# Squared score tiles kept in DRAM, turned, for the later query chunk of a two-batch attention and MLP kernel

## The chip, the cores and the metric

One core of one Trainium2 chip runs the whole program. The metric is the device time of one execution, in microseconds (us). It is given as the median of three runs; the profile is of one further execution.

## The reference

Shapes: two batches of 3136 rows, model width 256, query and key width 64, hidden width 1024. Everything is float32.

```
scores = (z @ z.T) / S                   # z: [2, 3136, 64], S = 3136; symmetric in query and key
attn   = maximum(scores, 0) ** 2         # so attn is symmetric too
x      = u * (attn @ v)                  # u, v: [2, 3136, 256]
h      = maximum(x @ w_in, 0)            # first MLP, 256 -> 1024
conv   = 3-tap convolution of h along the rows, one filter per hidden unit
x      = (h * sigmoid(conv)) @ w_out     # 1024 -> 256
xn     = (x - mean) / sqrt(var + 1e-6) * g_ln
out    = x + maximum(xn @ w1, 0) @ w2    # second MLP
```

## The kernel before

Each float32 operand of a matmul is kept as two float32r parts, a high part (`ah`, `vh`, ...) and the rest (`al`, `vl`, ...), and a product is the sum of two or three matmuls of such parts.

**Attention.** The 6272 queries of both batches are cut into 14 chunks of 448 (`WIDTHS`). A chunk goes over the 25 key tiles of its batch, 128 keys each; the last has 64 keys, whose high and low parts share one tile. For key tile j, `scores` issues two matmuls (L600, L601) into a PSUM tile `s` of 128 keys by 448 queries, ScalarE takes the positive part into the SBUF tile `a` (`relu`, L609), and ScalarE (L618) or in some tiles of the first four chunks VectorE (L614) squares it. ScalarE or VectorE then casts the high part `ah` (L382 and L386, lines of the helper `copy_r`) and VectorE subtracts for the low part `al` (L627). `av` adds attn times v into the PSUM tile `av`, for two halves of the model width with three matmuls each (L659, L661, L662). One key tile is thus eight matmuls of 448 columns, two of them for scores. At the chunk's end `gate_u` multiplies by u (L695).

**MLPs.** The rows are also cut into 17 blocks, 15 of 384 and two of 256 (`SIZES`). A block waits for the chunk that completes it. `mlps` goes over eight slices k of the hidden width: six matmuls up (L749 to L751), ScalarE and VectorE for the convolution, sigmoid and gate in a tile `t` (L790, L799, L807, L814, L819), the split into `gh` and `gl` (L829), and three matmuls down for each 128 rows (L765 to L767). Then come the normalisation (on PE the transposes L908) and the second MLP of the same form.

**Weights and loads.** All DMAs are issued from SyncE's queue (SP). `w_in`, `w_out`, `w1` and `w2` come as words that VectorE decodes in the first 200 us (L492 to L517); v and z are split in the same way (L474, L414). Each chunk loads its u and swaps two halves of z (`lh`, L565 and L566).

**Order.** A list scheduler, `Program`, sets the order. Every operation names its engine or engines with a planned duration, what it reads and writes, a due time, and the buffers it takes; buffers have a fixed number of places for each tag, and a buffer made with `True` as second argument is taken in the order of the program. The scheduler plays the whole kernel and emits each engine's instructions in the order it found. On the chip every queue, SP's too, runs in that order and waits at whatever is not there yet.

Of the kernel before, what the change touches and what calls it, by code (L numbers as in the profile page):

```python
# [15 lines left out]
P = 128  # L16
# [3 lines left out]
NJ = S // P + 1  # L20
ZW = NJ * P
EPS = 1e-6
WIDTHS = [448] * 7
SIZES = [3] * 15 + [2, 2]
WARM = 16
LAG0 = 70.0
# [8 lines left out]
GH = ("DVE", "ACT")  # L35
U_PLACES = 2
AH = ("ACT", "DVE")
CAPS = {"s": 3, "m": 3}
FUSED = 4, 2, 1
FLOAT = ("ACT", "POOL")  # L40
WH = ("ACT", "POOL")
VH = ("ACT", "POOL")
# [14 lines left out]
    "dve_copy": lambda n: 0.09 + 0.00048 * n,  # L57
    "dve_1": lambda n: 0.09 + 0.00048 * n,
    "dve_2": lambda n: 0.07 + 0.00108 * n,
    "dve_3": lambda n: 0.12 + 0.00108 * n,  # L60
    "pool_1": lambda n: 0.13 + 0.0009 * n,
    "pool_2": lambda n: 0.16 + 0.0026 * n,
# [200 lines left out]
def plan():  # L263

    chunks, blocks, after, q0, s = [], [], [], 0, 0
    for n in WIDTHS * NB:
        chunks.append((q0, q0 + n))  # L270
        q0 += n
    assert q0 == NT
    for n in SIZES:
        e = s + n * P
        blocks.append((s, e))
        after.append(next(c for c, (_, q1) in enumerate(chunks) if q1 > e or q1 == NT))
        s = e
    assert s == NT and set(after) == set(range(len(chunks)))
    return chunks, blocks, after
# [3 lines left out]
def attn_moe_kernel(ctx: ExitStack, tc: tile.TileContext, zt, ut, v, w_in, conv_w, w_out, g_ln, w1, w2, out):  # L283
# [10 lines left out]

    const = ctx.enter_context(tc.tile_pool(name="const", bufs=1))
    pool = ctx.enter_context(tc.tile_pool(name="work", bufs=1))
    psum = ctx.enter_context(tc.tile_pool(name="psum", bufs=1, space=PSUM))

    ident = const.tile([P, P], F32, name="ident")
# [14 lines left out]
    def maker(tag, places, where, shape, dtype):  # L314
# [5 lines left out]
    tags = {  # L320
        tag: maker(tag, places, where, shape, dtype)
        for tag, places, where, shape, dtype in (
            ("zst", 2, pool, [P, 512], F32),
            ("st", 3, pool, [P, 1024], F32),
            ("wc", 1, pool, [P, 512], U32),
            ("wn", 1, pool, [P, 512], U32),
            ("cst", 1, pool, [P, 3 * NF, 2], U32),
            ("chi", 1, pool, [P, 3 * NF], F32),
            ("clo", 1, pool, [P, 3 * NF], F32),
            ("a", 4, pool, [P, CW], F32),  # L330
            ("ah", A_PLACES, pool, [P, CW], F32R),
            ("al", A_PLACES, pool, [P, CW], F32R),
            ("lh", 2, pool, [P, CW], F32R),
# [1 line left out]
            ("xh", 1, pool, [P, 2 * XW], F32R),  # L335
            ("xl", 1, pool, [P, 2 * XW], F32R),
            ("h", 3, pool, [P, XW], F32),
            ("t", 3, pool, [P, BW], F32),
            ("gh", 3, pool, [P, BW], F32R),
            ("gl", 3, pool, [P, BW], F32R),  # L340
            ("ysb", 1, pool, [P, NTT * D], F32),
            ("xn", 3, pool, [P, D], F32),
            ("xth", 1, pool, [P, 2 * BW], F32R),
# [17 lines left out]
    def buf(tag, fixed=False, kind=None):  # L361
        if fixed:
            orders[tag] = orders.get(tag, 0) + 1
        return Buf(tag, orders[tag] if fixed else None, kind)
# [9 lines left out]
    def price(kind, n):  # L374
        return PRICE[kind](n)

    def f(ap):
        return ap.bitcast(F32)
# [11 lines left out]
        return [(e, us[e]) for e in (first, *others)]  # L390

    def dma(fn, kb, **kw):
        return op([("SP", max(0.08, kb / 190.0))], lambda e: fn(), late=2.0 + kb / 400.0, **kw)


    zp = [(o, min(o + 512, ZW)) for o in range(0, ZW, 512)]
# [189 lines left out]

    at_b = {}

    def scores(c, j, due):
        q0, q1 = chunks[c]  # L590
        n, o = q1 - q0, q0 % S
        ps, ab, lh = buf("w", kind="s"), buf("a"), lh_b[c]

        def a():
            return at(ab, "a")[:, :n]

        def mm(e):
            p = at(ps, "s")[:, :n]
            zj = hl[:, j * P : (j + 1) * P]
            nc.tensor.matmul(p, zj, hl[:, o : o + n], start=True, stop=False)  # L600
            nc.tensor.matmul(p, zj, at(lh)[:, :n], start=False, stop=True)  # L601

        lh_keys = [(lh, 0)] if c == 0 else [(lh, 0), (lh, 1)]
        op(
            [("PE", 2 * price("mm", n))], mm, reads=sorted({*hl_keys(j * P, P), *hl_keys(o, n)}) + lh_keys,
            writes=[(ps, 0)], takes=[ab], due=due, name=f"s{c}.{j}",
        )
        op(
            [("ACT", price("act_ps", n))], lambda e: nc.scalar.activation(a(), at(ps)[:, :n], AF.Relu),  # L609
            reads=[(ps, 0)], writes=[(ab, 0)], name="relu",  # L610
        )
        if c < FUSED[0] and j % FUSED[1] < FUSED[2]:
            op(
                [("DVE", price("dve_ps", n))], lambda e: nc.vector.tensor_tensor(a(), a(), at(ps)[:, :n], ALU.mult),  # L614
                reads=[(ps, 0)], writes=[(ab, 0)], name="square",
            )
        else:
            op([("ACT", price("act", n))], lambda e: nc.scalar.activation(a(), a(), AF.Square), writes=[(ab, 0)], name="square")  # L618
        ah, al = buf("ah"), buf("al") if j < NJ - 1 else None
        op(  # L620
            ways_copy(n, *AH), lambda e: copy_r(e, at(ah, "ah")[:, :n], a()),
            reads=[(ab, 0)], writes=[(ah, 0)], name="ah", port=True,
        )
        if al is not None:
            op(
                [("DVE", price("dve_2", n))],
                lambda e: nc.vector.tensor_tensor(at(al, "al")[:, :n], a(), f(at(ah)[:, :n]), ALU.subtract),  # L627
                reads=[(ab, 0), (ah, 0)], writes=[(al, 0)], name="al", port=True,
            )
        else:  # L630
            op(
                [("DVE", price("dve_2", n))],
                lambda e: nc.vector.tensor_tensor(
                    at(ah)[64:, :n], at(ab)[64:, :n], f(at(ah)[64:, :n]), ALU.subtract
                ),
                reads=[(ab, 0)], writes=[(ah, 0)], name="al", port=True,
            )
        at_b[c, j] = ah, al

    begun = set()  # L640

# [84 lines left out]
    def mlps(c, when):  # L726
# [201 lines left out]
        acc2 = shared("y") if tail else buf("y", True)  # L928
        for k in range(NF):
            ps = buf("w", kind="m")  # L930
            gh, gl = (buf("ah"), buf("al")) if beside else (buf("gh", True), buf("gl", True))
            for ways, fn, reads, due, d in up(ps, "w1", k, th, tl, n, when2(TURN + 0.02 + UP2 * k / NF)):
                op(ways, fn, reads=reads, adds=[(ps, 0)], takes=[gh, gl], due=due + 0.5 * d, name=f"h2{c}.{k}")
            op(
# [31 lines left out]
            pr.writers[k] = []  # L966

    note(("ident",))
    step = [(8 * price("mm", q1 - q0)) for q0, q1 in chunks]
    begin = [NJ * sum(step[:c]) for c in range(NC + 1)]  # L970
    lh_b[0] = buf("lh", True)
    load_z(0, 0, with_lh=lh_b[0])
    load_v(0, 0, 2)
# [6 lines left out]
        for i in range(4):  # L980
            load_w(nm, i)
    last0 = max(c for c in range(NC) if chunks[c][1] <= S)
    pace = 0.0
    for c in range(NC):
        if c == last0 + 1:
            for i in range(len(zp)):
                load_z(1, i)
            for a in range(0, NJ, 4):
                load_v(1, a, min(a + 4, NJ))
        if c:  # L990
            swap_lh(c)
        load_u(c)
        av_b[c] = buf("av", True)
        for j in range(NJ):
            t = 2 * (begin[c] + j * step[c])
            scores(c, j, t - 3.0)
            for d in range(2):
                av(c, j, d, t + d * 0.5)
        gate_u(c)
        for i in (i for i in range(NK) if after[i] == c):  # L1000
            make_x(i)
            length = (blocks[i][1] - blocks[i][0]) / NT * begin[NC]
            pace = max(pace, begin[c + 1])
            if c >= NC - 2:
                length = LENGTH[i - NK]
            lag = max(LAG1, LAG0 * (1 - c / LAG2))
            mlps(i, lambda x, pace=pace, lag=lag, length=length: 2 * (pace + lag + x * length))
            pace += length


    order = pr.order()
# [61 lines left out]
```

## Time and profile before

| what | value |
|---|---|
| median of three runs | 1152.42 us (1152.34 to 1155.17) |
| the profiled execution, its own time | 1152.26 us |
| its span, first to last instruction | 1150.3 us |
| PE (TensorE matmul) busy | 1136.2 us, 99% |
| VectorE (DVE) busy | 843.9 us, 73% |
| ScalarE (ACT) busy | 817.6 us, 71% |
| GpSimd (POOL) busy | 24.6 us, 2% |
| mean granted TensorE clock | 0.999 of full speed, the 2.4 GHz level |

Busy time is the time in which an engine has an instruction in work. Matmuls overlap in the engine, so the duration of one (0.36 us) is longer than the step from one start to the next (0.20 us); the steps are what add up. The span leaves out what lies before the first and after the last instruction, here 2.0 us.

### The profile page before, as it was taken

The page shows a single profiled execution, that of the slowest core. Times are in us where ns is not written, and L with a number is a line of the kernel's source. Part 1 is how long each engine was busy: PE and PEld are TensorE (multiplying, and loading weights), DVE is VectorE, ACT ScalarE, POOL GpSimd, SP SyncE. Part 2 cuts the span into 40 slices and gives each one's busy share as a digit, 9 for nine tenths or more (in the row PEclk, how much of TensorE's full clock was granted, in tenths as well). Part 3 has the DMA queues.
Part 4 walks back from the last instruction along what each step waited for, and adds up shares of the span by engine and source line. Part 5 has one row for each costly group of instructions (what it writes and reads, how often), then busy time and mean ns, then how long its engine had stood idle before and what let it go on. Part 6 is the DMA issues. An engine that isn't in the chain of part 4 may idle for free.

```text
span 1150.3 us, 18104 instructions
## 1 busy us (share of the span) xinstructions
PE 1136.2 (99%) x6870; PEld 1086.6 (94%) x6870; DVE 843.9 (73%) x1795; ACT 817.6 (71%) x1667; POOL 24.6 (2%) x39
## 2 busy tenths in 40 slices
PE   8999999999999999999999999999999999999998
PEld 7899999999999999999999999999999899999998
DVE  8999989948758596875848677775848576686694
ACT  7898878747767586776857667676858476785772
POOL 1000000000000000000000000000000000000000
PEclk9999999999999999999999999999999999999999
DMA  6412112100000021000000000000000000000000
GB/s 196 135 53 64 53 46 74 56 2 14 25 15 17 21 73 44 23 1 15 25 1 24 16 15 25 15 17 15 25 14 5 21 14 1 15 1 15 1 2 33
DMA packets 24823, 35.23 MB, mean 31 GB/s; under 512 B 1952, under 2 KB 20128, under 8 KB 24736
## 3 DMA queue, kind: packets, MB, share of 16 engines
q1 hardware_dynamic: 24736, 34.08, 9.8%
q8 instruction: 54, 0.88, 0.3%
q14 instruction: 33, 0.27, 0.1%
HBM read 24.67 MB, written 6.42 MB: 27 GB/s over the span
## 4 chain that ended last, share of the span: by engine, by line
PE 94%; DVE 2%; ACT 2%; issue 1%; DMA 0%; POOL 0%; DVEq 0%; POOLq 0%
PE av L659 12%; PE av L662 12%; PE av L661 11%; PE y L767 8%; PE y L765 8%; PE y L766 8%; PE s L600 5%; PE s L601 5%; PE h2ps L749 4%; PE h2ps L750 4%; PE h2ps L751 4%; PE hps L749 4%; PE hps L750 4%; PE hps L751 4%; PE tps L908 1%
## 5 line engine op out<-in xcount | busy, mean ns | idle before, releaser
L627 DVE TENSOR_TENSOR al<-a,ah 128x448 fp32r<-128x448 f32 x336 | 206.4, 622 | 90.6 <-ACT ah L382 88.2
L609 ACT ACTIVATE a<-s 128x448 f32<-128x448 f32 x350 | 185.0, 542 | 111.7 <-PE s L601 111.3
L659 PE MATMUL av<-ah,vh 128*128 128x448 f32 x700 | 258.2, 369 | 3.6 <-ACT ah L382 1.6
L662 PE MATMUL av<-ah,vl 128*128 128x448 f32 x700 | 253.8, 363 | 0.0
L661 PE MATMUL av<-al,vh 128*128 128x448 f32 x672 | 245.4, 365 | 2.7 <-DVE al L627 2.7
L618 ACT ACTIVATE a<-a 128x448 f32<-128x448 f32 x298 | 170.5, 580 | 4.0
L382 ACT CAST ah<-a 128x448 fp32r<-128x448 f32 x273 | 152.6, 568 | 6.7 <-DVE a L614 2.5
L659 PEld LDWEIGHTS av<-ah,vh 128*128 128x128 f32 x700 | 131.6, 188 | 14.3 <-ACT ah L382 3.2
L936 ACT ACTIVATE g2h<-h2ps 128x384 fp32r<-128x384 f32 (+1 forms) x136 | 65.1, 479 | 110.5 <-PE h2ps L751 106.3
L662 PEld LDWEIGHTS av<-ah,vl 128*128 128x128 f32 x700 | 131.6, 188 | 9.2
L941 DVE SCALAR_TENSOR_TENSOR g2l<-h2ps,g2h 128x384 fp32r<-128x384 f32 (+1 forms) x136 | 73.1, 540 | 89.2 <-ACT g2h L936 88.3
L661 PEld LDWEIGHTS av<-al,vh 128*128 128x128 f32 x672 | 126.5, 188 | 12.0 <-DVE al L627 5.9
L600 PE MATMUL s<-hl 128*128 128x448 f32 x350 | 128.3, 367 | 0.3 <-DVE hl L414 0.3
L601 PE MATMUL s<-lh,hl 128*128 128x448 f32 x350 | 128.0, 366 | 0.0
L765 PE MATMUL y<-w2h,g2h 128*128 128x256 f32 x392 | 110.5, 282 | 0.0
L767 PE MATMUL y<-w2h,g2l 128*128 128x256 f32 x392 | 110.2, 281 | 0.2 <-DVE g2l L941 0.2
L765 PE MATMUL y<-woh,gh 128*128 128x256 f32 x392 | 110.4, 282 | 0.0
L766 PE MATMUL y<-wol,gh 128*128 128x256 f32 x392 | 110.3, 281 | 0.0
L766 PE MATMUL y<-w2l,g2h 128*128 128x256 f32 x392 | 110.3, 281 | 0.0
L767 PE MATMUL y<-woh,gl 128*128 128x256 f32 x392 | 110.0, 281 | 0.0
L799 DVE SCALAR_TENSOR_TENSOR t<-h,cw,t 128x384 f32<-128x384 f32 (+1 forms) x136 | 81.7, 603 | 17.1 <-ACT t L790 16.1
L749 PE MATMUL hps<-xh,wih 128*128 128x386 f32 (+1 forms) x272 | 90.7, 333 | 0.7 <-DVE a L614 0.6
(113 smaller groups left out, 2283.7 us busy)
## 6 DMA issues: line engine op xcount, KB each, us to landing
u<-in_ut_dram SPq DMA_DIRECT2D x14, 448.0 KB, 3.6
out_dram<-ysb SPq DMA_DIRECT2D x15, 384.0 KB, 2.5
vst<-in_v_dram SPq DMA_DIRECT2D x11, 512.0 KB, 3.9
wst<-in_w_dram SPq DMA_DIRECT2D x8, 512.0 KB, 3.7
zst<-in_zt_dram SPq DMA_DIRECT2D x12, 256.0 KB, 2.9
lh<-hl SPq DMA_DIRECT2D x26, 112.0 KB, 2.8
wst<-in_w_in_dram SPq DMA_DIRECT2D x4, 512.0 KB, 3.8
wst<-in_w_out_dram SPq DMA_DIRECT2D x4, 512.0 KB, 3.6
```

What stands on the lines that cost most here:

```text
L600: nc.tensor.matmul(p, zj, hl[:, o : o + n], start=True, stop=False)
L601: nc.tensor.matmul(p, zj, at(lh)[:, :n], start=False, stop=True)
L609: [("ACT", price("act_ps", n))], lambda e: nc.scalar.activation(a(), at(ps)[:, :n], AF.Relu),
L618: op([("ACT", price("act", n))], lambda e: nc.scalar.activation(a(), a(), AF.Square), writes=[(ab, 0)], name="square")
L627: lambda e: nc.vector.tensor_tensor(at(al, "al")[:, :n], a(), f(at(ah)[:, :n]), ALU.subtract),
L659: nc.tensor.matmul(p, vhj, at(ah)[:, :n], start=first(b, d), stop=False, **kw)
L661: nc.tensor.matmul(p, vhj, at(al)[:, :n], start=False, stop=False, **kw)
L662: nc.tensor.matmul(p, vlj, at(ah)[:, :n], start=False, stop=False, **kw)
L749: nc.tensor.matmul(p, a, h_, start=d == 0, stop=False)
L765: nc.tensor.matmul(p, a, wh, start=first(acc, (i0 + i) // 2), stop=False, **kw)
L766: nc.tensor.matmul(p, a, wl, start=False, stop=False, **kw)
L767: nc.tensor.matmul(p, b, wh, start=False, stop=k == NF - 1, **kw)
```

## The change

The squared scores are symmetric: the tile of keys K by queries Q is the transpose of the tile of keys Q by queries K. Before, both are computed. The change makes chunks of whole key tiles: `TILES` gives 4, 4, 3, 4, 3, 3 and 4 tiles for the seven chunks of a batch, so 512, 512, 384, 512, 384, 384 and 448 queries (the last chunk ends with the half tile).

In chunk i, a key tile that lies in a later chunk is computed as before. In addition VectorE turns its `a` in blocks of 32 by 32 into a new tile `bl` (two places), and four DMAs on SP's queue (two for the half tile) write it to a DRAM tensor `turned`, each 32 keys as pieces of 32 elements (`spill`). A key tile that lies in an earlier chunk is not computed: one DMA reads 128 rows of `turned` into `a` (`land`, at most four at a time, `CAPS["ld"]`), and the two score matmuls, `relu` and the square are left out (`mirrored`). The cast, the subtraction and the six `av` matmuls stay. `turns` mixes the read tiles evenly with the computed ones. There are 146 spills (560 DMAs) and 154 landings in the kernel.

Besides, `a` has 6 places for 4 and its buffers, with `ah` and `al`, are taken in order; `st` has 2 for 3, `zst` 1 for 2, `t`, `gh` and `gl` 2 for 3 each. `FUSED` puts the square on VectorE in every fourth tile of the first two chunks, where it was every second of the first four. The scheduler's price of a DMA changes, and the blocks' operations are made after each chunk with the last three blocks at the end.

```diff
...
 NJ = S // P + 1
 ZW = NJ * P
 EPS = 1e-6
-WIDTHS = [448] * 7
+TILES = [4, 4, 3, 4, 3, 3, 4]
+SQ = 32
+MIRROR = 0
 SIZES = [3] * 15 + [2, 2]
 WARM = 16
 LAG0 = 70.0
...
 GH = ("DVE", "ACT")
 U_PLACES = 2
 AH = ("ACT", "DVE")
-CAPS = {"s": 3, "m": 3}
-FUSED = 4, 2, 1
+CAPS = {"s": 3, "m": 3, "ld": 4}
+FUSED = 2, 4, 1
 FLOAT = ("ACT", "POOL")
 WH = ("ACT", "POOL")
 VH = ("ACT", "POOL")
...
 
 
     chunks, blocks, after, q0, s = [], [], [], 0, 0
-    for n in WIDTHS * NB:
-        chunks.append((q0, q0 + n))
-        q0 += n
+    for b in range(NB):
+        for i in range(len(TILES)):
+            q1 = min(b * S + sum(TILES[: i + 1]) * P, (b + 1) * S)
+            chunks.append((q0, q1))
+            q0 = q1
     assert q0 == NT
     for n in SIZES:
         e = s + n * P
...
     tags = {
         tag: maker(tag, places, where, shape, dtype)
         for tag, places, where, shape, dtype in (
-            ("zst", 2, pool, [P, 512], F32),
-            ("st", 3, pool, [P, 1024], F32),
+            ("zst", 1, pool, [P, 512], F32),
+            ("st", 2, pool, [P, 1024], F32),
+            ("bl", 2, pool, [P, CW], F32),
...
-            ("a", 4, pool, [P, CW], F32),
+            ("a", 6, pool, [P, CW], F32),
...
-            ("t", 3, pool, [P, BW], F32),
-            ("gh", 3, pool, [P, BW], F32R),
-            ("gl", 3, pool, [P, BW], F32R),
+            ("t", 2, pool, [P, BW], F32),
+            ("gh", 2, pool, [P, BW], F32R),
+            ("gl", 2, pool, [P, BW], F32R),
...
 
     at_b = {}
 
+    per = len(TILES)
+    start_of = [sum(TILES[:i]) for i in range(per + 1)]
+    chunk_of = [i for i, n in enumerate(TILES) for _ in range(n)]
+
+    def mirrored(c, j):
+
+        b, i = divmod(c, per)
+        return chunk_of[j] < i and (b > 0 or chunk_of[j] >= MIRROR)
+
+    def spilled(c, j):
+        b, i = divmod(c, per)
+        return chunk_of[j] > i and mirrored(b * per + chunk_of[j], start_of[i])
+
+    turned = {}
+    for c in range(NC):
+        i = c % per
+        rows = S - start_of[i + 1] * P
+        if rows > 0:
+            turned[c] = dram.tile([P * TILES[i], rows], F32, tag=f"turned{c}", name="turned")
+
+    def spill(c, j, ab):
+        w = chunks[c][1] - chunks[c][0]
+        b = buf("bl")
+        op(
+            [("DVE", price("dve_turn", w))], lambda e: nc.vector.transpose(at(b, "bl")[:, :w], at(ab)[:, :w]),
+            reads=[(ab, 0)], writes=[(b, 0)], name="bl", port=True,
+        )
+        k0 = (j - start_of[c % per + 1]) * P
+
+        def write(e):
+            blocks_ = at(b)[:, :w].rearrange("p (b k) -> p b k", k=SQ)
+            for o in range(0, min(P, S - j * P), SQ):
+                dst = turned[c][:, k0 + o : k0 + o + SQ].rearrange("(b q) k -> q b k", q=SQ)
+                nc.sync.dma_start(out=dst, in_=blocks_[o : o + SQ])
+
+        op([("SP", 1.85)], write, reads=[(b, 0)], writes=[("turned", c, j)], late=2.2, due=1e4, name="spill")
+
+    def land(c, j):
+        q0, q1 = chunks[c]
+        n, i = q1 - q0, chunk_of[j]
+        src = c - c % per + i
+        k0 = (start_of[c % per] - start_of[i + 1]) * P
+        r0 = (j - start_of[i]) * P
+        b = buf("a", True, kind="ld")
+        op(
+            [("SP", 0.7)],
+            lambda e: nc.sync.dma_start(out=at(b, "land")[:, :n], in_=turned[src][r0 : r0 + P, k0 : k0 + n]),
+            late=2.4, writes=[(b, 0)], name="land",
+            reads=[("turned", src, jj) for jj in range(start_of[c % per], start_of[c % per + 1])],
+        )
+        return b
+
     def scores(c, j, due):
         q0, q1 = chunks[c]
-        n, o = q1 - q0, q0 % S
-        ps, ab, lh = buf("w", kind="s"), buf("a"), lh_b[c]
+        n = q1 - q0
+        from_dram = mirrored(c, j)
+        ab = land(c, j) if from_dram else buf("a", True)
 
         def a():
             return at(ab, "a")[:, :n]
+
+        if not from_dram:
+            products(c, j, ab, a, due)
+        ah, al = buf("ah", True), buf("al", True) if j < NJ - 1 else None
+        op(
+            ways_copy(n, *AH), lambda e: copy_r(e, at(ah, "ah")[:, :n], a()),
+            reads=[(ab, 0)], writes=[(ah, 0)], name="ah", port=True,
+        )
+        if spilled(c, j):
+            spill(c, j, ab)
...
+        at_b[c, j] = ah, al
+
+    def products(c, j, ab, a, due):
+        q0, q1 = chunks[c]
+        n, o = q1 - q0, q0 % S
+        ps, lh = buf("w", kind="s"), lh_b[c]
 
         def mm(e):
             p = at(ps, "s")[:, :n]
...
             )
         else:
             op([("ACT", price("act", n))], lambda e: nc.scalar.activation(a(), a(), AF.Square), writes=[(ab, 0)], name="square")
...
-        at_b[c, j] = ah, al
 
     begun = set()
 
...
             pr.writers[k] = []
 
     note(("ident",))
-    step = [(8 * price("mm", q1 - q0)) for q0, q1 in chunks]
-    begin = [NJ * sum(step[:c]) for c in range(NC + 1)]
+
+    def work(c, j):
+        n = chunks[c][1] - chunks[c][0]
+        return (6 if mirrored(c, j) else 8) * price("mm", n)
+
+    def turns(c):
+
+        old = [j for j in range(NJ) if mirrored(c, j)]
+        new = [j for j in range(NJ) if not mirrored(c, j)]
+        both = [((i + 1) / (len(x) + 0.5), x is old, j) for x in (old, new) for i, j in enumerate(x)]
+        return [j for *_, j in sorted(both)]
+
+    lengths = [sum(work(c, j) for j in range(NJ)) for c in range(NC)]
+    begin = [sum(lengths[:c]) for c in range(NC + 1)]
     lh_b[0] = buf("lh", True)
     load_z(0, 0, with_lh=lh_b[0])
     load_v(0, 0, 2)
...
             swap_lh(c)
         load_u(c)
         av_b[c] = buf("av", True)
-        for j in range(NJ):
-            t = 2 * (begin[c] + j * step[c])
+        t0 = begin[c]
+        for j in turns(c):
+            t = 2 * t0
+            t0 += work(c, j)
             scores(c, j, t - 3.0)
             for d in range(2):
                 av(c, j, d, t + d * 0.5)
         gate_u(c)
         for i in (i for i in range(NK) if after[i] == c):
-            make_x(i)
             length = (blocks[i][1] - blocks[i][0]) / NT * begin[NC]
             pace = max(pace, begin[c + 1])
             if c >= NC - 2:
                 length = LENGTH[i - NK]
             lag = max(LAG1, LAG0 * (1 - c / LAG2))
-            mlps(i, lambda x, pace=pace, lag=lag, length=length: 2 * (pace + lag + x * length))
+            when[i] = lambda x, pace=pace, lag=lag, length=length: 2 * (pace + lag + x * length)
             pace += length
+        for i in (i for i in when if i < NK - 3 and after[i] == c):
+            make_x(i)
+            mlps(i, when[i])
+    for i in range(NK - 3, NK):
+        make_x(i)
+        mlps(i, when[i])
 
 
     order = pr.order()
```

## Rows read from the trace of the kernel before

**Rows 1.** Page, part 1: busy time, share of the span, instructions.
```profile
PE 1136.2 (99%) x6870; PEld 1086.6 (94%) x6870; DVE 843.9 (73%) x1795; ACT 817.6 (71%) x1667; POOL 24.6 (2%) x39
```

**Rows 2.** Windows: length, busy (count) of PE, PEld, DVE, ACT, POOL; clock, DMA share, GB/s.
```profile
0.00:14.00 14.00, 11.22 (x50) 9.83 (x51) 9.93 (x18) 9.36 (x17) 1.58 (x9) 1.00 0.64 204
14.00:60.00 46.00, 43.12 (x205) 37.71 (x205) 44.50 (x93) 37.24 (x77) 1.80 (x3) 1.00 0.49 147
60.00:230.00 170.00, 168.97 (x944) 159.40 (x943) 160.99 (x338) 143.08 (x296) 4.44 (x6) 1.00 0.19 58
230.00:1100.00 870.00, 866.65 (x5300) 833.93 (x5299) 596.56 (x1262) 604.98 (x1221) 15.29 (x19) 1.00 0.06 17
1100.00:1150.30 50.30, 46.19 (x378) 45.77 (x377) 31.97 (x90) 22.88 (x59) 1.50 (x2) 0.98 0.06 20
```

**Rows 3.** Waits of PE: longest in total first; us, times, longest.
```profile
PE av L661 <- DVE al L627: 2.7, 7, 0.5
PE av L659 <- ACT ah L382: 1.6, 3, 0.7
```

**Rows 4.** Timeline near 61 us: start, us, engine, line, operation.
```profile
60.48 0.36 PE L600 MATMUL s<-hl 128*128 128x448 f32 x1
...
61.49 0.36 PE L601 MATMUL s<-lh,hl 128*128 128x448 f32 x1
...
61.69 0.34 PE L749 MATMUL hps<-xh,wih 128*128 128x386 f32 x1
...
63.63 0.34 PE L751 MATMUL hps<-xh,wil 128*128 128x386 f32 x1
```

**Rows 5.** Groups by line and shape: busy us, mean ns; idle before, releaser.
```profile
L609 ACT ACTIVATE a<-s 128x448 f32<-128x448 f32 x350 | 185.0, 542 | 111.7 <-PE s L601 111.3
L618 ACT ACTIVATE a<-a 128x448 f32<-128x448 f32 x298 | 170.5, 580 | 4.0
L627 DVE TENSOR_TENSOR al<-a,ah 128x448 fp32r<-128x448 f32 x336 | 206.4, 622 | 90.6 <-ACT ah L382 88.2
L614 DVE TENSOR_TENSOR a<-a,s 128x448 f32<-128x448 f32 x52 | 31.8, 617 | 3.2 <-ACT a L609 3.1
L386 DVE CAST ah<-a 128x448 fp32r<-128x448 f32 x77 | 30.5, 397 | 26.5 <-ACT a L618 25.3
```

**Rows 6.** The same view, 256-row blocks: first and last of seven groups.
```profile
L790 ACT ACTIVATE t<-h,cw 128x256 f32<-128x256 f32 x16 | 8.1, 508 | 0.3
...
L829 DVE TENSOR_TENSOR gl<-t,gh 128x256 fp32r<-128x256 f32 x16 | 6.3, 421 | 0.2
```

**Rows 7.** DMA in the window 449.5:450.4: packets; queue, MB, share of 16 engines.
```profile
DMA packets 144, 0.07 MB, mean 73 GB/s; under 512 B 16, under 2 KB 144, under 8 KB 144
q1 hardware_dynamic: 144, 0.07, 24.9%
```

**Rows 8.** The same in the window 264.4:266.0, one store of `ysb`.
```profile
DMA packets 400, 0.39 MB, mean 246 GB/s; under 512 B 16, under 2 KB 400, under 8 KB 400
q1 hardware_dynamic: 400, 0.39, 73.8%
```

**Rows 9.** Page, parts 3 and 6: the queue over the span; issues, KB, us to landing.
```profile
q1 hardware_dynamic: 24736, 34.08, 9.8%
...
out_dram<-ysb SPq DMA_DIRECT2D x15, 384.0 KB, 2.5
...
zst<-in_zt_dram SPq DMA_DIRECT2D x12, 256.0 KB, 2.9
```

**Rows 10.** Timeline of SP's queue: start, us, line of the issue.
```profile
468.46 0.49 SPq L565 DMA_DIRECT2D lh<-hl  x1
469.00 0.59 SPq L566 DMA_DIRECT2D lh<-hl  x1
```

**Rows 11.** Waits of SP's queue: us, times, longest.
```profile
SPq L955 <- DVE ysb L949: 533.0, 15, 70.9
```

**Rows 12.** Timeline of DVE: the gates that end the first two chunks.
```profile
52.68 1.16 DVE L695 SCALAR_TENSOR_TENSOR u<-av,u 128x448 f32<-128x448 f32 x2
...
103.30 1.16 DVE L695 SCALAR_TENSOR_TENSOR u<-av,u 128x448 f32<-128x448 f32 x2 [0.17 <-PE av L662]
```

## What the change does to the time: the prediction

> **What bounds the kernel now.** I read the page's busy shares first, then the windows by stage, then what PE waits for, then a stretch of the timeline, and last the transfers. PE is busy for 99% of the span, at the full clock, VectorE for 73% and ScalarE for 71% [rows 1]. By stage: PE is idle for 2.8 us of the first 14 and 2.9 us of the next 46, for about 1 us up to 230, for 3 us of the 870 after that, and for 4 us at the end [rows 2]. The longest waits of PE on one line come to 2.7 us [rows 3]. A busy PE could still be a waiting one, so the step from one start to the next decides. Six score matmuls of 448 columns start 1.01 us apart from first to last, five steps of 0.202 us; twelve of 386 columns need 1.94 us, eleven steps of 0.176 us [rows 4]. That is (0.202 - 0.176)/62 = 0.41 ns for each column more, and nothing stands between the matmuls. So PE's own work sets the end, and a matmul left out is worth its whole step, unless something new makes PE wait.
>
> VectorE is nearly as full in one place: up to 230 us it is busy 9.9 + 44.5 + 161.0 = 215.4 us, 94%, and ScalarE 189.7 us, 82%; from 230 to 1100 us they stand at 69% and 70% [rows 2]. In the first stage v, z and the weights are split beside the attention. The new work must pass there.
>
> **What it removes.** In chunk i the tiles of the earlier chunks are read: 0, 4, 8, 11, 15, 18, 21 tiles of 512, 512, 384, 512, 384, 384, 448 columns, 77 tiles and 32,832 columns for a batch, 154 and 65,664 in all, 426 columns on average. Each saves two matmuls of 0.202 - 22 x 0.00041 = 0.193 us: 308 x 0.193 = 59.4 us of PE. The other matmuls keep their number and their total of columns, since there are still seven chunks of 25 tiles. ScalarE loses relu and square of those columns, (542 + 580)/448 = 2.50 ns each [rows 5], 164 us, and takes over 39 squares (52 before, 13 after) of 0.58 us, 23 us. It is not the bound, so this counts as nothing.
>
> **What VectorE gains.** 146 turns: the spilled tiles of a batch are 21, 17, 10 of 512 and 14, 7, 4 of 384, together 68,352 columns in the kernel. The trace has no such instruction. The cheapest row that reads and writes a tile of this size is the cast, 397/448 = 0.89 ns a column, a subtraction costs 622/448 = 1.39 [rows 5]. I take 1.39, since nothing says that a turn goes at the cast's faster rate: 95 us (61 at the cast's). Nothing bounds it above; for the range I double it, 190. The squares give back 32 - 9 = 23 us. So VectorE comes to 844 + 95 - 23 = 916 us of some 1100, 83%: enough on the average.
>
> The Trainium skill (VectorE: DVE Perf Modes, The three transpose paths) gives 311 ns for a 128x128 bf16 turn on VectorE in blocks of 32. By its 2.43 ns a column the turns would come to an estimated 166 us, 31 us more of them in the first stage, and the sum below to an estimated 1137 at most; no row here shows one.
>
> In the first stage, up to 230 us, lie the first four chunks. Their turns: 48 tiles of 512 and 14 of 384, 29,952 columns, 42 us; the squares give back 23 us. VectorE's 215 us become 234, less up to 8 us of casts that ScalarE could take, where PE would need 230 less the 10 us saved in these chunks (23 tiles read, 10,752 columns, two matmuls at 0.45 ns). VectorE is over by 6 to 14 us. Part can be put off, because MLP work may run later, where VectorE has room. PE has nothing to fill chunk 0 with, as no MLP runs until its gate is done (at 52.7 us before [rows 12], with the first MLP matmul at 61.7 [rows 4]).
>
> **Behind the turns.** A place of `bl` is held for the turn (0.7 us), four issues at 0.54 us each from start to start [rows 10] and a landing of about 2.5 us like a store's [rows 9]: 5.4 us, so two places pass a tile every 2.7 us. Chunk 0 has 21 spills, 57 us, against 198 matmuls of 0.228 us = 45 us and about 14 us of start. When `bl` is full, the next turn waits on VectorE; behind it stand the subtractions of the next tiles, and PE waits for those. Six places of `a` take up part of it. For both effects, which overlap, I take 10 us, between 0 and 25.
>
> **The transfers.** A spilled tile of 512 columns is 2,048 pieces of 128 bytes, 128 for each of the 16 engines; all spills are 262,656 pieces. The trace shows larger packets: 144, mostly of 512 bytes, took 0.249 x 0.9 us x 16/144 = 25 ns each [rows 7], 400 of 1 KB, a store, 0.738 x 1.6 x 16/400 = 47 ns [rows 8]. The line through both gives 8 ns at 128 bytes. Bounds are 8 and 47; I take 15, between the line and the nearest row. Then a tile costs 1.9 us of all engines, the spills 246 us. With the landings (33.6 MB, as much as the 34.1 MB that now take 9.8% of the engines [rows 9]) the share rises from 10% to about 42%. Chunk 0 needs 20.5 x 1.9 = 39 us of its 59: hidden. At 25 ns it needs 66 us, 7 us too many, which the 10 above hold.
>
> SP issues 560 + 154 DMAs more at 0.54 us, 386 us of 1100. Its queue waits long today, up to 71 us for an `ysb` [rows 11], with little behind it. Now spills and landings stand behind such waits. A landing has four places, and 256 KB land in 2.9 us [rows 9], less than the 3.3 us that a tile and its share of MLP take (1150 us, 14 chunks of 25 tiles). I take 0, and up to 10 us in the range.
>
> **Fewer places.** With two places of `t`, `gh`, `gl` for three, a slice k of a 256-row block takes 3.13 us from the first tap to `gl` (seven groups, the first 508, the last 421 ns [rows 6]), so one slice in 1.57 us, and PE needs 12 matmuls of about 0.12 us, 1.44. Beside attention this is covered; in the last 50 us, 16 slices lose 2 us and the waits between engines something: 3 us, 0 to 8. `zst` and `st` with a place less delay loads in the first stage only; that is in the 10.
>
> **Sum.** Profiled execution 1152.3 (span 1150.3 and 2.0 around it; the median, 1152.4, is the same). 1152.3 - 59.4 + 10 + 3 = 1105.9, so 1106 us, 4.0% faster. With every loss at its lower end 1093; with 25, 10 and 8 us lost, 1136.
>
> **Rivals.**
> 1. *VectorE is the bound for a quarter of the kernel.* If a turn costs twice 1.39 ns a column, the first stage gets 42 us more on an engine that is already over. At chunks 7 and 8 (38 tiles, then 54 us of turns in some 180 us) 30% come on top of 69%. Of the 42 us I take 30 as lost and 5 at chunks 7 and 8: 1106 + 35 = 1141. For it: 94% before 230 us. Against it: the scheduler may put MLP work off.
> 2. *Slower: the small pieces choke the DMA engines.* The place is `bl` in the chunks that spill most. At 47 ns a piece, chunk 0 needs 123 us of the engines against 59, chunk 1 99 against about 56 (it took 51 with 448 columns [rows 12]), chunk 2 61 against 50, chunk 7 123 against 94 (82 x 512/448), chunk 8 99 against 92: 64 + 43 + 11 + 29 + 7 = 154 us lost in place of the 10, time 1250. It decides from about 36 ns on, where chunks 0 and 1 lose 35 + 20 us, which with the 3 of the end eat the 59. For it: no row shows a store of pieces under 1 KB. Against it: rows 7 and 8 fall with size, 47 to 25 ns. The Trainium skill (DMA: Bandwidth & Descriptors, Specifications) says that under 512 bytes the engine reads, modifies and writes; by that rule this rival holds; no row here shows a store of so small pieces.
> 3. *No change.* The 59 us come back as PE waits because the turn stays in step with the landings, for instance when a landing waits on SP behind an `ysb` and the due tile is missing: 154 landings late by 0.38 us each suffice. Time 1152. Against it: four landings may be ahead.
>
> **Chances.** Forecast, 1090 to 1128: 0.60. Rival 1, 1128 to 1149: 0.18. Rival 2: 0.14, nearly all slower. Rival 3: 0.04. Better than 1090, if the idle 14 us of today shrink too: 0.04. Faster by over 0.3% (about 3.5 us, what a measurement of this kernel can tell from no change) is 0.60 + 0.18 + 0.04 = 0.82, the same 0.04, slower 0.14. The range 1086 to 1149 holds the first two and a little of the last. Likeliest: 1106.
>
> **What would show it.** Right: PE's busy time falls by some 59 us and its share stays at 97% or more; the turns' group shows about 0.65 us on average and 95 us in all; DMA packets rise by about 280,000, their share to about 42%; waits of PE grow only before 60 us. Wrong: turns of more than 1 us; a spill's landing of more than 5 us, with the turns waiting on DMA and PE on subtractions in chunks 0, 1 and 7; waits of PE on casts that wait for `land`; PE idle in the last 50 us growing by more than 8 us.

## The result and the profile after

The changed kernel takes 1124.62 us (median of four runs, 1124.1 to 1126.58) against 1152.41 before: ratio 0.9756, 95% interval 0.9738 to 0.9775. That is faster, by 28 us and not the 46 forecast. Its profiled execution took 1126.58 us, of which the span is 1124.6.

The page's busy shares, the DMA engines' queue, and the chain that ended last, followed back from the last instruction through what each step waited for (by engine, then by line):

```profile
PE 1091.6 (97%) x6562; PEld 1018.9 (91%) x6562; DVE 867.1 (77%) x1835; ACT 715.2 (64%) x1460; POOL 30.8 (3%) x44
...
DMA packets 318622, 102.52 MB, mean 91 GB/s; under 512 B 276032, under 2 KB 307904, under 8 KB 318528
...
q1 hardware_dynamic: 318528, 101.33, 39.7%
...
PE 76%; DVE 9%; DMA 7%; ACT 4%; SPq 2%; issue 2%; DVEq 0%; POOL 0%; ACTq 0%
PE av L729 9%; PE av L732 9%; PE av L731 9%; PE y L837 7%; PE y L835 7%; PE y L836 7%; PE h2ps L819 4%; PE h2ps L820 4%; PE h2ps L821 4%; PE hps L819 3%; PE hps L821 3%; PE hps L820 3%; DMA turned<-bl 3%; SPq L629 2%; PE s L691 2%
```

PE has 308 matmuls fewer than in [rows 1], as planned, but its busy time fell by 44.6 us only, and its share from 99% to 97%. The chain holds two new links: the spills' transfers and their issues on SP (L629), 3% and 2% of the span. They crowd at the start: in the part of the chain up to 100 us the spills' landings are 22% and their issues 13%.

Windows of the stages that [rows 2] show, in the same columns (length, busy of PE, PEld, DVE, ACT, POOL, clock, DMA share, GB/s):

```profile
0.00:14.00 14.00, 10.05 (x41) 8.18 (x42) 9.56 (x16) 8.84 (x15) 1.99 (x10) 1.00 0.81 249
14.00:60.00 46.00, 38.69 (x146) 28.43 (x145) 39.51 (x74) 30.83 (x59) 5.28 (x9) 0.93 0.78 166
60.00:230.00 170.00, 161.32 (x809) 137.08 (x808) 159.36 (x322) 134.53 (x268) 5.29 (x6) 1.00 0.73 154
```

PE is idle for 4.0, 7.3 and 8.7 us here, where it was idle for 2.8, 2.9 and 1.0. In the second the clock fell too.

**Counting without the stalls.** PE's idle time rose by 18.9 us, from 14.1 to 33.0, but that is not all that is lost: a matmul at half the clock, for one, counts as busy for longer (0.63 us for 0.40 in the stall shown below). So I count PE's own work: each matmul its step, on the line through the two steps of [rows 4], 0.0087 + 0.000431 us a column (0.109 us for a transpose). A stretch's length less the own work of the matmuls that start in it is its loss, whatever the reason. Own work was 1126.3 us before and is 1067.0 now: 59.3 us less. Loss rose from 24.0 to 57.6 us. By stage, in us (medians are those of the timed runs; the rest comes from each kernel's one profile):

| kernel | median | ratio, 95% interval | loss 0–100 | 100–180 | 180–240 | to end − 125 | last 125 |
|---|---|---|---|---|---|---|---|
| before | 1152.41 | 1 | 11.0 | 0.7 | 0.7 | 6.0 | 5.6 |
| after | 1124.62 | 0.9756 (0.9738–0.9775) | 27.8 | 4.4 | 4.4 | 6.0 | 15.0 |
| e1_land4 | 1121.78 | 0.9725 (0.9707–0.9743) | 15.8 | 1.5 | 11.4 | 7.6 | 15.0 |
| e2_no_turn | 1122.30 | 0.9728 (0.9713–0.9742) | 22.9 | 4.8 | 4.0 | 5.6 | 15.0 |
| e5_land4_no_turn | 1101.12 | 0.9550 (0.9533–0.9567) | 13.5 | 0.7 | 0.1 | 3.5 | 15.5 |
| e11_split | 1129.68 | 0.9799 (0.9781–0.9817) | 22.0 | 12.2 | 3.3 | 7.0 | 15.6 |
| e12_split_no_turn | 1129.06 | 0.9781 (0.9761–0.9800) | 18.9 | 13.9 | 6.6 | 7.8 | 15.8 |
| e8_true_prices | 1123.94 | 0.9749 (0.9733–0.9765) | 30.4 | 3.6 | 1.8 | 4.2 | 15.0 |
| e3_mirror1 | 1124.07 | 0.9724 (0.9699–0.9750) | 12.4 | 5.2 | 8.4 | 5.4 | 14.5 |
| e4_before_places | 1157.87 | 1.0043 (1.0029–1.0057) | 11.0 | 2.2 | 0.4 | 4.7 | 9.7 |
| e6_tail_t | 1122.62 | 0.9741 (0.9724–0.9758) | 25.3 | 3.9 | 3.1 | 4.6 | 15.2 |
| e7_land4_tail | 1122.41 | 0.9738 (0.9722–0.9753) | 16.9 | 1.3 | 10.2 | 7.7 | 16.2 |
| e9_late_last | 1112.58 | 0.9647 (0.9629–0.9665) | 27.6 | 3.9 | 3.0 | 4.0 | 5.3 |
| e10_all | 1113.07 | 0.9655 (0.9630–0.9679) | 18.5 | 1.5 | 9.1 | 4.4 | 8.7 |

The loss of after against before: 24.2 us more up to 240 us (36.6 for 12.4), where I had put 10, nothing in the middle, and 9.4 us more at the end, where I had put 3. One of the four runs of e3 took 1192.55 us at a lower clock; its ratio leaves that run out, its median does not.

**One stall, step by step.** SP's queue around 40 us (start, duration from the first issue to the end of the last, line, tile, count):

```profile
34.41 4.32 SPq L629 DMA_DIRECT2D turned<-bl  x8
38.83 0.45 SPq L538 DMA_DIRECT2D wst<-in_w_in_dram  x1
39.38 2.14 SPq L629 DMA_DIRECT2D turned<-bl  x4
41.62 1.57 SPq L413 DMA_DIRECT2D zst<-in_zt_dram  x1
43.28 0.38 SPq L538 DMA_DIRECT2D wst<-in_w_in_dram  x1
43.72 5.41 SPq L629 DMA_DIRECT2D turned<-bl  x8
49.24 0.45 SPq L540 DMA_DIRECT2D wst<-in_w_out_dram  x1
```

The four issues of a spill take 2.14 us of the queue, as long as 9 matmuls of 512 columns. The weight load of 38.83 us stands directly behind eight of them. It landed 4.4 us after its issue (such loads took 3.8 us before, 4.3 in after, medians), so the transfer is little of its lateness. What VectorE did with it, then PE:

```profile
43.24 0.43 DVE L509 TENSOR_SCALAR wn<-wst 128x512 uint32<-128x512 uint32 x1 [1.85 <-DMA wst<-in_w_in_dram]
43.71 0.69 DVE L510 SCALAR_TENSOR_TENSOR wn<-wst,wn 128x512 uint32<-128x512 uint32 x1
44.32 0.68 DVE L704 TENSOR_TENSOR a<-a,s 128x512 f32<-128x512 f32 x1
```

```profile
41.63 0.40 PE L690 MATMUL s<-hl 128*128 128x512 f32 x1
41.87 0.39 PE L691 MATMUL s<-lh,hl 128*128 128x512 f32 x1
45.80 0.73 PE L729 MATMUL av<-ah,vh 128*128 128x512 f32 x1 [3.54 <-ACT ah L389]
...
48.06 0.63 PE L729 MATMUL av<-ah,vh 128*128 128x512 f32 x1
48.49 0.63 PE L731 MATMUL av<-al,vh 128*128 128x512 f32 x1
```

VectorE's decoding waits 1.85 us for the load; the square of L704 that is next in its order waits with it, then ScalarE's cast, then PE for 3.54 us. That is not all. Two windows of after, the stall and what follows it:

```profile
42.20:45.80 3.60, 0.06 (x2) 0.04 (x1) 2.49 (x6) 2.46 (x5) 0.00 (x0) 1.00 0.93 189
45.80:52.70 6.90, 6.38 (x14) 4.68 (x15) 6.74 (x13) 3.45 (x7) 0.00 (x0) 0.51 0.91 192
```

When PE starts again, the clock is granted at 0.51, the 1.2 GHz level, for 6.9 us: steps of 0.43 us for 0.23 at 41.63, with PE "busy" for 6.38 us. Fourteen steps at 0.20 us too much are 2.8 us: the wait of 1.85 us on VectorE, with 1.1 us of decoding behind it, has become 3.54 + 2.8 = 6.3 us of PE.

### The profile page after: what moved, and what is told of

Read it like the earlier page. It is cut to its first block, busy times and chain, and to the rows that moved or that the text cites. A ratio compares the mean times of both kernels' runs of the same rounds, so it can differ in the third digit from the quotient of the medians.

```text
span 1124.6 us, 18722 instructions
## 1 busy us (share of the span) xinstructions
PE 1091.6 (97%) x6562; PEld 1018.9 (91%) x6562; DVE 867.1 (77%) x1835; ACT 715.2 (64%) x1460; POOL 30.8 (3%) x44
## 3 DMA queue, kind: packets, MB, share of 16 engines
q1 hardware_dynamic: 318528, 101.33, 39.7%
## 4 chain that ended last, share of the span: by engine, by line
PE 76%; DVE 9%; DMA 7%; ACT 4%; SPq 2%; issue 2%; DVEq 0%; POOL 0%; ACTq 0%
PE av L729 9%; PE av L732 9%; PE av L731 9%; PE y L837 7%; PE y L835 7%; PE y L836 7%; PE h2ps L819 4%; PE h2ps L820 4%; PE h2ps L821 4%; PE hps L819 3%; PE hps L821 3%; PE hps L820 3%; DMA turned<-bl 3%; SPq L629 2%; PE s L691 2%
## 5 line engine op out<-in xcount | busy, mean ns | idle before, releaser
L729 PE MATMUL av<-ah,vh 128*128 128x512 f32 (+2 forms) x700 | 259.0, 370 | 10.6 <-ACT ah L389 6.7
L731 PE MATMUL av<-al,vh 128*128 128x384 f32 (+2 forms) x672 | 248.8, 370 | 7.5 <-DVE al L669 7.3
L732 PE MATMUL av<-ah,vl 128*128 128x512 f32 (+2 forms) x700 | 255.8, 365 | 0.0
L699 ACT ACTIVATE a<-s 128x512 f32<-128x512 f32 (+2 forms) x196 | 106.7, 557 | 73.9 <-PE s L691 71.5
L669 DVE TENSOR_TENSOR al<-a,ah 128x512 fp32r<-128x512 f32 (+2 forms) x182 | 114.8, 636 | 12.8 <-ACT ah L389 11.4
L620 DVE STREAM_TRANSPOSE bl<-a 128x512 f32<-128x512 f32 (+1 forms) x146 | 96.0, 659 | 23.5 <-ACT a L708 15.2
L389 ACT CAST ah<-a 128x512 fp32r<-128x512 f32 (+2 forms) x182 | 104.3, 581 | 5.7 <-DVE a L704 1.9
L708 ACT ACTIVATE a<-a 128x512 f32<-128x512 f32 (+2 forms) x183 | 106.0, 591 | 2.0
L669 DVE TENSOR_TENSOR al<-land,ah 128x384 fp32r<-128x384 f32 (+2 forms) x154 | 90.4, 594 | 11.6 <-ACT ah L389 11.1
L860 ACT ACTIVATE t<-h,cw 128x384 f32<-128x384 f32 (+1 forms) x136 | 82.0, 603 | 23.0 <-DVE gl L899 21.7
```

The lines of the kernel that those rows point to most:

```text
L389: nc.scalar.copy(dst, src)
L620: [("DVE", price("dve_turn", w))], lambda e: nc.vector.transpose(at(b, "bl")[:, :w], at(ab)[:, :w]),
L729: nc.tensor.matmul(p, vhj, at(ah)[:, :n], start=first(b, d), stop=False, **kw)
L731: nc.tensor.matmul(p, vhj, at(al)[:, :n], start=False, stop=False, **kw)
L732: nc.tensor.matmul(p, vlj, at(ah)[:, :n], start=False, stop=False, **kw)
L860: lambda e, h=h, t=t, k=k: nc.scalar.activation(at(t, "t")[:, :n], at(h)[:, :n], AF.Copy, scale=cw[:, k, 0:1]),
```

## The experiments

Theories, as the expectations name them. For the start: **A**, SP issues too slowly for four DMAs a spill; **A'**, the DMA engines are the limit, with 128-byte pieces; **B**, VectorE is full; **D**, it is writing the small pieces that is slow, not reading them. For the end: **C**, two places of `t`, `gh` and `gl` are too few; **E**, the order leaves too much MLP work for when the attention is over.

### The start

**e1_land4** turns the pieces round: the spill is one DMA of whole rows, and the landing gathers 128-byte pieces in four.

```
 turned[c] = dram.tile([(NJ - start_of[i + 1]) * P, width], ...)
 spill:  nc.sync.dma_start(out=turned[c][k0 : k0 + m, :], in_=at(b)[:m, :w])      # price 0.6
 land:   for o in range(0, P, SQ):                                               # price 2.15
             part = turned[src][k0 : k0 + n, r0 + o : r0 + o + SQ].rearrange("(x q) k -> q x k", q=SQ)
             nc.sync.dma_start(out=land[o : o + SQ, :n].rearrange("q (x k) -> q x k", k=SQ), in_=part)
```

> A spilled tile is written by one DMA of whole rows and read back by four DMAs of 128-byte pieces, so SP issues 1 for 4 in a spill and 4 for 1 in a landing; the turns on VectorE stay. In chunk 0 SP issues 21 spill DMAs in place of 82. Theory A (SP's issue rate is what is late in the first 240 us: weight loads stand behind spill issues, the decode waits on VectorE and PE behind it): the 33 us that PE loses up to 240 us (24 more than before) fall by at least 10, time 1108 to 1115. Theory B (VectorE is full in the first stage): turns unchanged, so nothing changes, 1122 to 1128. Theory D (pieces of 128 bytes written to DRAM are slow themselves): writes are now long pieces, so packets get shorter in time and bl's waits on DMA vanish; the time falls as in A, but the share of the DMA engines falls below 35%.

**e2_no_turn** keeps the four issues and the small pieces and drops the turn (`b = ab`).

> The turn is left out: the spill writes the unturned tile straight from a, so the later chunks get untransposed weights; the DMAs, their number and size stay. VectorE loses 96 us of work. Theory A (SP): the loss up to 240 us stays within 5 us, time 1117 to 1124. Theory B (VectorE): the loss up to 240 us falls by 10 or more, time 1105 to 1114.

Measured: 1121.78 and 1122.30. Neither gives the start back alone. e2 is what A forecast. e1 is not: its loss up to 240 us fell by 7.8 us and its time lies next to what B forecast. D fails too: the share of the DMA engines is 38.2%, not below 35%, and by the trace's packet records a piece of 128 bytes takes 13 ns of an engine read back (e1) as written (after). e1 takes 14.9 us off the loss up to 180 us and meets 7.0 more from 180 to 240; e2 takes 4.9 off up to 240. What e1 met, in windows of it:

```profile
0.00:100.00 100.00, 91.23 (x382) 70.52 (x383) 91.69 (x167) 77.69 (x147) 9.63 (x21) 1.00 0.62 194
180.00:200.00 20.00, 18.48 (x72) 14.39 (x72) 20.00 (x40) 16.35 (x31) 0.00 (x0) 0.91 0.78 186
```

PE does 382 matmuls in the first 100 us for 328 in after. But from 180 to 200 us VectorE is busy for 20.00 of 20 us: the decoding of `w1` and `w2`, put off so far, meets the turns there. That stretch itself loses 3.7 us; the other 7.7 are lost from 200 to 240 us, where VectorE is busy for 29.6 of 40 us and the clock is 0.91 on average; what holds PE there was not followed. Without the turns both go, as the next run shows.

**e5_land4_no_turn** has both edits. (Without the turn a spill goes straight from `a`, so e2 and e5 also drop the two places of `bl`.)

> The one-DMA spill of e1 and the left-out turn of e2 together (the later chunks get untransposed weights). With SP relieved, e1 lost 17 us up to 180 us but 11 us between 180 and 240, where VectorE is busy without a gap from 140 on. If VectorE's turns are the second limit there (A first, then B), the loss between 180 and 240 falls to 3 or less and the time to 1105 to 1113. If something else is late there (the small read pieces, the order), the time stays at 1117 to 1124.

Measured: 1101.12, 23.5 us below after and below the range expected, more than the two steps of 2 to 3 us together. The loss up to 240 us is 14.3, nearly that of before (12.4). So two limits stand one behind the other: taking one away shows the other. Which resource is the first, SP (A) or the DMA engines (A')? e1 changed both. So **e11_split** is e1 with the spill cut into four DMAs of 32 whole rows each, and **e12_split_no_turn** is that without the turn: long pieces, but again four issues.

```
 for o in range(0, m, SQ):                                                       # price 1.85
     nc.sync.dma_start(out=turned[c][k0 + o : k0 + o + SQ, :], in_=at(b)[o : o + SQ, :w])
```

> As e1, but each spill is again four DMAs, now of 32 whole rows each: SP issues four times a spill, as the changed kernel does, and the pieces written are 2 KB long, as in e1. Theory A (SP's issue rate): the loss up to 100 us goes from 15.8 in e1 back to 22 or more (27.8 in the changed kernel), time 1122 to 1128. Theory A' (the 16 DMA engines, 73 to 84% busy with 128-byte pieces in the first 100 us, 53 to 60% in e1): the loss up to 100 us stays at 14 to 18, time 1118 to 1123.

> e11 with the turn left out (the later chunks get untransposed weights), so that VectorE is no limit: e5 with four issues for one. Theory A: the loss up to 240 us goes from 14.3 in e5 back towards 31.7 (e2), to 22 or more, time 1109 to 1120. Theory A': it stays at 14 to 18, time 1100 to 1106.

Measured: 1129.68 and 1129.06. The windows 0:100 and 100:240, of e5_land4_no_turn and then of e12_split_no_turn:

```profile
0.00:100.00 100.00, 93.15 (x394) 73.76 (x395) 85.23 (x158) 77.44 (x148) 13.34 (x24) 0.98 0.71 214
100.00:240.00 140.00, 139.84 (x800) 130.03 (x799) 128.84 (x277) 107.02 (x219) 7.58 (x6) 1.00 0.61 144
```

```profile
0.00:100.00 100.00, 91.44 (x365) 69.45 (x366) 75.11 (x137) 66.09 (x124) 8.69 (x19) 0.98 0.64 174
100.00:240.00 140.00, 129.30 (x657) 112.41 (x656) 117.98 (x246) 102.26 (x205) 4.41 (x6) 0.96 0.64 149
```

The same bytes in the same pieces, no turns in either, and the number of issues per spill (with the price that the scheduler is given for them) makes 28 us. In the first 100 us the DMA engines are busier in the faster kernel (0.71 against 0.64), and VectorE in neither is full. So it is not the DMA engines' load that sets the time here (A'), nor VectorE (B), nor the writing of small pieces (D): it is SP's issues, together with the order that the scheduler makes for them. e11 says the same up to 180 us: with long pieces and four issues it loses 34.2 us, after 32.2, e1 17.3.

Three things stay open. Both kernels are slower than A forecast, and the 28 us are not what after pays: landings take four issues here as well, so SP issues 1282 DMAs in e11 and e12, 820 in after and 868 in e5. The price that the scheduler is given, and so its order, changed with the number of issues, and no run kept the one order with the other number, or issued the spills from a second queue. And up to 100 us e11 loses 22.0 us, at the lower edge of what A forecast, and after 27.8, with four issues for a spill in both: that difference goes with the small pieces or with the order.

The pair also shows the order of the two limits: with one issue per spill, dropping the turns gains 21 us (e1 to e5), with four, nothing (e11 to e12).

**e8_true_prices** asks whether the scheduler was only told wrong: spill 2.16 us for 1.85, turn 0.06 + 0.00111n for 0.06 + 0.001n.

> Only the scheduler's durations of two operations are set to what the profile of the changed kernel shows: 2.16 us of SP for the four issues of a spill (1.85 before) and 0.63 us from start to start for a turn of 512 columns (0.57). Instructions are the same, their order differs. Theory A says that the order was made for an SP that is faster than the real one, so that weight loads end up behind spills: the loss up to 100 us falls by 5 or more, time 1114 to 1120. Rival (SP's work itself is too much there, whatever the order): the loss only moves, 1122 to 1128.

Measured: 1123.94, as the rival said, the loss up to 240 us 35.8 for 36.6. With the right prices the work on SP is the same, and the order that the scheduler makes of them doesn't hide it.

**e3_mirror1** (`MIRROR = 1`) computes the tiles of the first batch's chunk 0 anew, so that chunk 0 spills nothing.

> The first chunk of the first batch spills nothing and no tile of it is read back: 21 spills (82 DMAs) and 21 turns fewer in chunk 0, and 4 tiles in each of six chunks are computed again, 10,496 columns, two matmuls at 0.45 ns, 9.4 us more of PE. Theories A and B both: the 17 us that PE loses more than before up to 100 us fall to about 3, so -14 + 9 = 1119, between 1115 and 1123. If the loss up to 100 us is from the fewer places of zst and st or from other loads, it stays and the time is 1133.

Measured: 1124.07, just above what was expected. The loss up to 100 us falls from 27.8 to 12.4, near the 11.0 of before, so it is chunk 0's spills and not the fewer places of `zst` and `st`; own work grows by 9.5, and 100 to 240 us lose 4.8 more. The place is right, the trade gains next to nothing.

### The end

**e4_before_places** is the kernel before with two places of `t`, `gh` and `gl` for three. **e6_tail_t** is after with `t` from the six places of `a` in the last blocks (`t = buf("a") if tail else buf("t")`); **e7_land4_tail** is e1 with the same.

> The kernel before with only t, gh and gl at two places in place of three. Theory C (the fewer places cost PE time once the attention is over, at 1040 to 1060 us in the changed kernel): the last 110 us grow by 8 to 10 us, 1160 to 1163. Rival (the loss there is from the order of the last blocks, not from places): 1151 to 1155.

> The changed kernel, in which the last two blocks take their tile t from the six places of a, which the attention no longer needs; gh and gl keep two places. Theory C (two places of t hold the tap back: ScalarE's L860 waits for VectorE's gl): the loss from 1000 us on falls by 4 to 8, time 1117 to 1121. Rival (gh and gl, or VectorE itself, set the pace there): 1123 to 1126.

> The spill in one DMA (e1) and t of the last two blocks from a (e6) in one kernel. If both gains add: 1121.8 less 4 to 8, 1114 to 1118. If the end is paced by VectorE alone: 1120 to 1123.

Measured: before loses 4.1 us more at its end with two places and 5 us in all, less than expected. But a third and more places of `t` give after nothing there: 15.2 and 16.2 us for 15.0 (1122.62 and 1122.41 in all, the second as expected if VectorE alone paces the end). So places can cost something in before's order, and `t`'s are not what costs in after's; `gh` and `gl` were not tried.

The gates that end the chunks, of after (count; min, median, max ns; first and last start), and then a window of after behind the last of them:

```profile
L765 DVE SCALAR_TENSOR_TENSOR u<-av,u x28: 548/618/694, 71.8 to 1018.4; 128x512 f32<-128x512 f32 x12, 128x384 f32<-128x384 f32 x12, 128x448 f32<-128x448 f32 x4
```

```profile
1040.00:1060.00 20.00, 15.50 (x109) 13.85 (x108) 18.14 (x50) 12.61 (x30) 0.96 (x1) 0.99 0.01 1
```

In after the attention ends 106 us before the end of the span; before, the last gate started at 1085.1 us, 65 us before it. In what follows the gates PE had 91.4 us of own work left in after, 60.7 before. There are only MLP steps then, and by this window VectorE paces them: it is busy for 18.14 of 20 us where PE is busy for 15.50. **e9_late_last** makes the attention of the last three chunks due later, by 20, 40 and 60 in the scheduler's units, and nothing else, so that MLP work goes between:

```
-            t = 2 * t0
+            t = 2 * t0 + (20 * max(0, c - NC + 4))
```

> The changed kernel with one edit in the due times: the attention of the last three chunks is due 20, 40 and 60 us later, so that more MLP work stands beside it. In the changed kernel the last gate is done at 1018 us and 91 us of PE work, all MLP, is left for the last 102 us (before: 61 of 61). Theory E (the order leaves too much MLP work without attention beside it, and VectorE paces that): the last gate moves 15 us or more closer to the end, the loss of the last 125 us falls from 15 to 8 or less, time 1113 to 1119. Rival (two places of t, gh and gl cost it wherever the work stands): the loss stays at 13 to 16, time 1122 to 1126.

Measured: 1112.58, 12.0 us below after. By the two profiles, whose spans lie 13.7 us apart, 9.7 us are won in the last 125 us and 4.0 before. Its gates, and the last 125 us of after and then of e9_late_last:

```profile
L765 DVE SCALAR_TENSOR_TENSOR u<-av,u x28: 547/618/694, 72.4 to 1042.9; 128x512 f32<-128x512 f32 x12, 128x384 f32<-128x384 f32 x12, 128x448 f32<-128x448 f32 x4
```

```profile
999.60:1124.60 125.00, 115.10 (x830) 111.40 (x828) 84.17 (x216) 61.46 (x144) 3.31 (x4) 0.99 0.03 11
```

```profile
985.90:1110.90 125.00, 120.56 (x868) 117.77 (x867) 84.80 (x206) 66.10 (x154) 2.35 (x3) 1.00 0.08 27
```

The last gate starts 68 us before the end, and the loss there is 5.3 us, that of before (5.6), with two places of `t`, `gh` and `gl`. E is shown, C is not needed.

**e10_all** joins e1, the turn's price of e8, no square on VectorE in the first two chunks (`FUSED = 0, 4, 1`), and later dues by 15, 30 and 45.

> One DMA for a spill and four for a landing (e1), the planned durations of e8 for the turn, attention of the last three chunks due 15, 30 and 45 us later (as in e9), and all squares on ScalarE, which takes 9 us of the first stage from VectorE. If SP, VectorE and the order of the end are the three causes of what is missing, the loss up to 240 us falls from 37 to 22 to 26 and that of the last 125 us to 8 or less: 1104 to 1111. If one of them was only moved, 1113 to 1120.

Measured: 1113.07, above what was expected and no better than e9. Its last 125 us lose 8.7, e9's 5.3. Up to 240 us it still loses 29.1: 9.1 from 180 on, where VectorE is busy for 38.5 of the first 40 us. The version to keep is e9, 3.5% below before.

## Why the prediction was half right

**What is removed** came as worked out: 59.3 us of own work for 59.4. Its check, PE's busy time falling by 59, was badly chosen: the page read 44.6, since slow steps count as busy. The step from [rows 4] would have told it.

**The turns** came as worked out. The groups of after, by shape (busy, mean ns, idle before):

```profile
L620 DVE STREAM_TRANSPOSE bl<-a 128x512 f32<-128x512 f32 x96 | 67.4, 705 | 19.7 <-ACT a L708 12.8 <-DMA turned<-bl 6.6
L620 DVE STREAM_TRANSPOSE bl<-a 128x384 f32<-128x384 f32 x50 | 28.6, 573 | 3.8 <-ACT a L708 2.5 <-DMA turned<-bl 0.9
```

96.0 us for 95, 705/512 = 1.38 ns a column for 1.39; rival 1 (twice as much) is out. The Trainium skill's 311 ns for a 128x128 bf16 turn (VectorE: DVE Perf Modes, The three transpose paths), carried over to these float32 tiles by columns, would have made an estimated 166 us; the measurement decides.

**The pieces** cost less than I took. The queue's time is 0.397 x 1124.6 x 16 = 7144 us of an engine; before it was 0.098 x 1150.3 x 16 = 1804, and the landings, as many bytes as all of before's traffic, take about as much again. What is left, some 3,500 us over 262,656 pieces, is an estimated 13 ns each, for 15, and the packet records of the trace give the same (mean 12.9 ns); the share is 39.7% for 42. Rival 2 needed 36 ns. The Trainium skill says that under 512 bytes the engine reads, modifies and writes (DMA: Bandwidth & Descriptors, Specifications); no run here shows that as a cost: 13 ns lie far under the 36 that rival 2 needs, and the pieces take as long when they are read back in e1.

**The step that failed** is "SP issues 560 + 154 DMAs more at 0.54 us, 386 us of 1100 ... I take 0, and up to 10 us in the range". The 0.54 us were right (L629: 2.14 us for four), the average of a third of the span was no argument: in the first 100 us the loads of weights, v and z share the queue with the spills of the chunks that spill most, in one order. I had looked for what stands behind a landing, and not for what stands behind a spill: a weight load, the decoding on VectorE that waits for it, a square behind that. So the 10 us for `bl` and VectorE became 24, and SP's issues come first among their causes, as far as e5 and e12 show it. The path that the prediction did name is there too: a place of `bl` is held through the four issues and the landing, and the chain runs through both (13% and 22% up to 100 us), though VectorE stood idle for a full `bl` for only 7.5 us in the whole kernel. VectorE being over in the first stage was right, as the second limit: e5 shows it.

**The end** was a size that was off, for another cause than named: 9.4 us for 3, above the 8 of its range, and not from the places but from the order, with 91 us of MLP work behind the last gate in place of 61. Most likely the last chunks, whose score matmuls are gone, were over sooner; the change also makes the last three blocks' operations after all chunks, and no run separates the two. I counted what the change removes from the last chunks and never asked what was left to run beside them.

**Waits of PE grow only before 60 us** was wrong: they grow up to 240 us and at the end. Rival 3's place, landings late in the middle, took nothing: 6.0 us lost in both.

Sum, for the profiled execution: 1105.9 + 14.2 at the start + 6.4 at the end = 1126.5; measured 1126.58. That the time still lies in the forecast's range, near its upper end, is luck in part: the 25 us allowed for `bl` and VectorE covered a loss whose first cause was put at nothing.

What stays open: how to get the start back with the turns. e5, without turns, lies 21 us below e1, and what e9 wins at the end lies elsewhere (e5 still loses 15.5 there, e9 5.3). If turns could be hidden wholly, both together would make an estimated 1101 - 10 = 1091 us; no run shows that.

## What to carry to other kernels

Count a queue's issues in the stage where they crowd and list what stands behind each in the queue's order; a share over the whole span hides it (SP issues for a third of the span in all, but for 71% of the first 100 us). Where a change makes one kind of work shorter, look at what was running beside it, since an order that was balanced for the longer one can leave the other over at the end. And read PE's work by steps, not by busy time, and expect a limit behind the one that you take away.

## What the runs showed of the hardware

A DMA that stores 64 KB in 512 pieces of 128 bytes landed 2.0 us (median) after its issue; the same 64 KB in rows of 2 KB took 1.7 us (e11), and 256 KB in such rows 2.1 us (e1). A piece of 128 bytes took 13 ns of a DMA engine, written (after) or read (e1). Four issues took SP 2.14 us. One stall of TensorE of 3.5 us was followed by 6.9 us at the 1.2 GHz level, which cost 2.8 us more.
